# Elementwise work moved from VectorE to GpSimd, and squares from ScalarE to VectorE, in a gated-loop attention with a mixture-of-experts layer

## The chip, the core and the metric

The kernel runs on one core of one Trainium2 chip. The metric is device time in microseconds (us) of one execution, the median of several. The core has five engines with a queue each: TensorE (PE in the profile; PEld are its weight loads), VectorE (DVE), ScalarE (ACT), GpSimd (POOL) and SyncE (SP, which here only issues DMAs).

## What is computed

Two layers follow each other. The first is a recurrence over 768 steps with a complex decay per channel, for 4 batches and 8 heads of 48 channels; the second sends each of the 3072 tokens to one of 8 experts.

```python
mag = np.sqrt(a_re * a_re + a_im * a_im)
scale = np.minimum(mag, 0.999) / (mag + 1e-06)
a_re_n, a_im_n = (a_re * scale, a_im * scale)
for t in range(S):
    new_re = ar * S_re - ai * S_im
    new_im = ar * S_im + ai * S_re
    kv = np.einsum('bhd,bhe->bhde', k[:, :, t], v[:, :, t])
    S_re, S_im = (new_re + kv, new_im)
    y[:, :, t] = np.einsum('bhd,bhde->bhe', q[:, :, t], S_re)
...
logits = x @ w_gate + modality_bias[modality_id]
e_idx = np.argmax(logits, axis=1)
...
h = np.maximum(x[mask] @ w1[e], 0.0)
out[mask] = gate_w[mask, None] * (h @ w2[e])
```

## The kernel before

The recurrence is done in chunks of 128 steps: 6 chunks of each of 4 batches are 24 units, taken two at a time as 12 *pairs* (index x, `NX` = 12; a unit of the pair is `w`, `NU` = 24, and unit w is chunk `w // 4` of batch `w % 4`). A tile of a pair has 128 steps on the partitions and 2 × 8 × 48 = 768 channels in a row, in fp32.

For each pair, the decays become a phase and a log-modulus, both summed over the steps of the chunk by matmuls with triangular matrices. The steps are functions:

- `load_a` loads a_re and a_im into `abs_`, which holds two pairs.
- `squares` makes `sq` = the squares of both (ScalarE, L135, recorded at the helper's line L107 as `sq<-abs`, 1536 elements), `tan` = a_re·a_im (VectorE, L137), `neg` = the sign of a_re as bf16 (L139), and the sum of the squares (L140).
- `logs` and `tangents`: logarithms and exponentials on ScalarE; VectorE multiplies `tan` (L159) and clips `lm` (L160). `arctans` follows on ScalarE.
- `angles`: TensorE sums `tan` and `neg` into `u` (L172, L173). `fractions`: VectorE reduces it to a fraction of a turn (`f` and `r`, L193 to L202; L193 reads PSUM). `waves`: ScalarE makes sine and cosine into `css`.
- `sums` and `moduli`: TensorE sums the log-moduli, ScalarE makes `pm`, the exponential of the sum and of its negative.

For each unit, `hats` scales k and q by `pm` into `qkp` (L253) and multiplies that with the waves into `QK` (L257, 1536 elements); `turned` transposes QK on TensorE and copies it out on ScalarE (L275); `inner` makes the masked products `W` (L291, from PSUM), and the state of the recurrence: `mid` = old state + first half (L302), `U` = mid + second half (L307), both reading PSUM, and the next state = U times the chunk's decay `mt` (L309). `outer` and `rows` make the output rows and router logits (`lg`, L345). The state of a unit is read by the unit four later, the next chunk of its batch.

The loop over w (L399) writes these steps interleaved: pair x + 5 is squared while pair x + 3 gets its waves and unit w goes through `outer`. Instructions are put on the engines by a scheduler that keeps this order roughly; ScalarE's activations are kept in an exact order by `act` and `table` (L98 to L107), since each change of function table costs a load (L104). Each engine takes its queue in order. From the ninth unit on the router is made in between; from the 19th, the expert layer's first tiles. GpSimd issues the scatters of rows by token (L639, `x_slots`) and later those of the output (L885); SyncE issues the other transfers. Before 159 us of the profile GpSimd has only memsets and constants, all within the first 10 us.

Of the kernel before, what the change touches and what calls it, by code (L numbers as in the profile page):

```python
# [11 lines left out]
F32 = mybir.dt.float32  # L12
BF16 = mybir.dt.bfloat16
AX = mybir.AxisListType
Alu = mybir.AluOpType
# [8 lines left out]
def gate_loop(nc, ctx, tc, cpool, ident, q, k, v, a_re, a_im, sel, lg, x_rows, make_router, make_layers):  # L24
# [100 lines left out]
    def load_qk(x):  # L125
        qk = io.tile([L, 2, NG, H, D], F32, name="qk")
        for i, (g, b) in enumerate(groups[x]):
            nc.sync.dma_start(out=qk[:, 1, i], in_=at(q, g, b))
            nc.sync.dma_start(out=qk[:, 0, i], in_=at(k, g, b))
        box["qk", x] = qk  # L130

    def squares(x):
        ab = box.pop(("ab", x))
        sq = el.tile([L, 2, NG, H, D], F32, name="sq", bufs=1)
        act(sq[:], ab, Act.Square)  # L135
        tan = el.tile([L, NG, H, D], F32, name="tan", bufs=2)
        nc.vector.tensor_tensor(tan[:], ab[:, 0], ab[:, 1], Alu.mult)  # L137
        neg = el.tile([L, NG, H, D], BF16, name="neg", bufs=2)
        nc.vector.tensor_scalar(neg[:], ab[:, 0], 0.0, None, Alu.is_lt)  # L139
        nc.vector.tensor_tensor(sq[:, 1], sq[:, 0], sq[:, 1], Alu.add)  # L140
        box["squares", x] = sq, tan, neg
# [100 lines left out]

    def hats(w):

        if not 0 <= w < NU or (hats, w) in done:
            return
        done.add((hats, w))
        x, i = w // NG, w % NG
        cs = box["cs", x]
        pm = box["pm", x]  # L250
        qk = box["qk", x]
        qkp = un.tile([L, 2, H, D], F32, name="qkp", bufs=1)
        nc.vector.tensor_tensor(qkp[:], qk[:, :, i], pm[:, :, i], Alu.mult)  # L253
        QK = QKs[w % 4]
        wave = cs[:, i].rearrange("p h c d -> p (h c d)")[:, None, :].broadcast_to([L, 2, H * 2 * D])
        twice = qkp[:].rearrange("p a h d -> p (a h) d")[:, :, None, :].broadcast_to([L, 2 * H, 2, D])
        box["hat"] = nc.vector.tensor_tensor(QK[:, :, :, :, 0:D].rearrange("p a h c d -> p (a h c) d"), wave, twice, Alu.mult)  # L257
        box["hats", order[w]] = QK
# [22 lines left out]
    def inner(g, b):  # L281
# [23 lines left out]
        if more:  # L305
# [3 lines left out]
            nc.vector.tensor_tensor(new[:], U[:], box["mt", (g * B + b) // NG][:, b % NG, :, None].broadcast_to([C, H, D]), Alu.mult)  # L309
# [89 lines left out]
    for w in range(-4, NU + 1):  # L399
# [20 lines left out]
        if even:  # L420
# [6 lines left out]
            phase(moduli, x + 2)  # L427
            phase(logs, x + 4)
# [600 lines left out]
```

## Time and profile before

| | us |
|---|---|
| time before, median of 3 runs | 338.72 (337.75 to 339.82) |
| the profiled execution's own time | 337.64 |
| its span in the profile | 336.0 |
| busy: TensorE matmuls | 260.6 |
| busy: VectorE | 238.1 |
| busy: ScalarE | 235.6 |
| busy: GpSimd | 73.6 |
| mean granted TensorE clock | 0.938 |

The span is what the trace covers; the execution's own time is 1.6 us more. A row of a group gives the line, the engine, the operation, output and inputs with partitions × elements, the count, and after the bar the busy time in us and the mean of one in ns; then the idle time before it, with what ended that. A row of a timeline begins with its start and its duration in us. VectorE's and ScalarE's durations overlap a little with the next instruction's. A row of the view by stretches gives start and end, length, busy time and count of each engine, then the granted clock.

### The profile page before, as it was taken

What the parts mean: (1) busy time and instruction counts of PE and PEld (TensorE: products, weight loads), DVE (VectorE), ACT (ScalarE), POOL (GpSimd) and SP (SyncE); (2) the same over time, 40 slices, a digit from 0 to 9 for tenths busy, and PEclk for the clock granted to TensorE, in tenths of its full rate; (3) what the DMA queues carried; (4) which work ended last, traced back from release to release, by engine and by line L of the source; (5) the groups of instructions that cost most, each with busy time, mean ns of one, the idle gap of its engine ahead of it and who ended that gap; (6) DMA issues with size and microseconds to landing.
All of it is one profiled execution on the core that took longest, in us unless ns stands there. A gap on an engine that the chain in (4) does not pass through costs nothing.

```text
span 336.0 us, 13516 instructions
## 1 busy us (share of the span) xinstructions
PE 260.6 (78%) x5876; PEld 202.7 (60%) x5876; DVE 238.1 (71%) x437; ACT 235.6 (70%) x291; POOL 73.6 (22%) x110
## 2 busy tenths in 40 slices
PE   0034769789879798797958879899699999999960
PEld 0011448648478676676756667788678767676730
DVE  1719899999998989999897868978424373446510
ACT  2786999899998999979796978555333546542420
POOL 8100000000000000000333122324016267833440
PEclk9998596979998999997999999799989999999995
DMA  8996877869989878787989872463823441445320
GB/s 133 187 187 105 165 153 120 143 88 154 191 149 177 168 133 179 133 166 150 196 172 195 152 158 60 72 128 76 111 49 94 113 142 61 130 112 129 87 93 7
DMA packets 172157, 43.83 MB, mean 130 GB/s; under 512 B 162978, under 2 KB 168484, under 8 KB 172088
## 3 DMA queue, kind: packets, MB, share of 16 engines
q1 hardware_dynamic: 166456, 32.60, 55.3%
q0 software_dynamic: 5632, 10.26, 12.5%
q8 instruction: 48, 0.79, 1.0%
q14 instruction: 21, 0.17, 0.1%
HBM read 33.96 MB, written 9.77 MB: 130 GB/s over the span
## 4 chain that ended last, share of the span: by engine, by line
PE 42%; DVE 18%; ACT 14%; issue 9%; DMA 7%; SPq 6%; POOL 1%; POOLq 0%; DVEq 0%; ACTq 0%
PE h_ps L849 9%; PE y_ps L869 7%; PE wp L290 5%; PE up L298 4%; PE yp L327 4%; DVE QK L257 3%; ACT sq L107 3%; PE xw L339 2%; PE u L172 2%; PE ls L218 2%; ACT L104 2%; ACT pm L107 2%; PE tQT L274 2%; PE yp L321 2%; PE tKT L274 2%
## 5 line engine op out<-in xcount | busy, mean ns | idle before, releaser
L639 POOL DMA_INDIRECT x_slots<-xr,to x24 | 30.6, 1276 | 215.8 <-DMA mt<-m_scr 149.3
L172 PE MATMUL u<-tan,turn 128*128 128x384 f32 x48 | 24.3, 594 | 23.8 <-ACT tan L107 23.6
L257 DVE TENSOR_TENSOR QK<-css,qkp 128x1536 f32<-128x1536 f32 x24 | 42.1, 1755 | 0.4
L849 PE MATMUL h_ps<-xgT,w1t 128*128 128x256 bf16 (+1 forms) x312 | 36.8, 274 | 0.3 <-DMA xgT<-x_slots 0.3
L869 PE MATMUL y_ps<-w2t,hT 128*128 128x384 bf16 x200 | 35.7, 326 | 0.8 <-ACT hT L852 0.3
L885 POOL DMA_INDIRECT out_dram<-y_sb,idx x25 | 26.7, 1070 | 29.9 <-ACT y_sb L883 15.6
L849 PEld LDWEIGHTS <-w1t 128*128 128x128 bf16 x312 | 29.8, 100 | 5.6 <-issue 0.5
L104 ACT ACT_TABLE_LOAD x25 | 32.1, 1283 | 1.4 <-PEq L1013 0.9
L290 PE MATMUL wp<-QT,KT 128*64 128x64 f32 x768 | 30.8, 239 | 2.4 <-issue 1.7
L298 PE MATMUL up<-V,QK 64*64 64x48 f32 x1408 | 30.6, 234 | 2.3 <-DVE W L291 1.6
L290 PEld LDWEIGHTS wp<-QT,KT 128*64 128x64 f32 x768 | 27.2, 150 | 8.6 <-issue 2.8
L883 ACT ACTIVATE y_sb<-y_ps,own 128x384 f32<-128x384 f32 x25 | 13.2, 578 | 26.3 <-PE y_ps L869 18.3
L275 ACT COPY KT<-tKT 128x1024 f32<-128x1024 f32 x24 | 24.3, 1012 | 9.5 <-PE tKT L274 9.5
L298 PEld LDWEIGHTS up<-V,QK 64*64 64x64 f32 x1408 | 27.7, 149 | 4.3 <-DVE W L291 1.7
L852 ACT ACTIVATE hT<-h_ps 128x1024 bf16<-128x1024 f32 (+1 forms) x20 | 20.1, 1003 | 14.4 <-PE h_ps L849 14.4
L274 PE MATMUL tKT<-ident,QK 64*128 64x64 f32 x384 | 18.4, 240 | 13.0 <-DVE QK L257 10.6
L274 PEld LDWEIGHTS tKT<-ident,QK 64*128 64x128 f32 x384 | 15.2, 149 | 20.0 <-issue 16.5
L869 PEld LDWEIGHTS <-hT 128*128 128x128 bf16 x200 | 18.0, 98 | 14.6 <-DVE hT L854 2.4
L172 PEld LDWEIGHTS u<-tan,turn 128*128 128x128 f32 x48 | 9.2, 218 | 28.5 <-issue 26.0
L328 ACT COPY yT<-yp 128x512 f32<-128x512 f32 x24 | 14.0, 584 | 17.5 <-PE yp L327 17.3
L275 ACT COPY QT<-tQT 128x1024 f32<-128x1024 f32 x24 | 24.5, 1021 | 0.0
L253 DVE TENSOR_TENSOR qkp<-qk,pm 128x768 f32<-128x768 f32 x24 | 22.8, 952 | 0.3 <-ACT pm L107 0.3
(153 smaller groups left out, 542.2 us busy)
## 6 DMA issues: line engine op xcount, KB each, us to landing
abs<-in_a_re_dram SPq DMA_DIRECT2D x24, 192.0 KB
abs<-in_a_im_dram SPq DMA_DIRECT2D x24, 192.0 KB
qk<-in_q_dram SPq DMA_DIRECT2D x24, 192.0 KB
qk<-in_k_dram SPq DMA_DIRECT2D x24, 192.0 KB
V<-in_v_dram SPq DMA_DIRECT2D x24, 192.0 KB
cb<-f_scr SPq DMA_DIRECT2D x10, 384.0 KB
x_rows<-xr SPq DMA_DIRECT2D x24, 96.0 KB
abs<-in_moe_w_dram POOLq DMA_DIRECT2D x2, 768.0 KB, 8.9
```

The lines of the kernel that those rows point to most:

```text
L104: then(nc.scalar.preload_act_table_set(name))
L172: nc.tensor.matmul(us[:, i], turn[:], tan[:, i], start=True, stop=False)
L253: nc.vector.tensor_tensor(qkp[:], qk[:, :, i], pm[:, :, i], Alu.mult)
L257: box["hat"] = nc.vector.tensor_tensor(QK[:, :, :, :, 0:D].rearrange("p a h c d -> p (a h c) d"), wave, twice, Alu.mult)
L274: nc.tensor.transpose(tp[:, s, h], QK[rows_, i, h].rearrange("t c d -> t (c d)"), ident[rows_, rows_])
L275: box["turned QK"] = nc.scalar.copy(to[:], tp)
L290: nc.tensor.matmul(wp[rows_, h, :], KT[:, s, h], QT[:, s, h], start=True, stop=True)
L298: nc.tensor.matmul(up[to_c, s, h], QK[rows_, 0, h, c], V[rows_, h, 0:D], start=True, stop=True)
L639: put = self.nc.gpsimd.indirect_dma_start(out=self.x_slots, out_offset=bass.IndirectOffsetOnAxis(ap=to, axis=0), in_=self.xr[m // 4 * 4][: ...
L849: nc.tensor.matmul(h_ps[:, f // nf, f % nf, :], w1t[:, k, ff * 128:(ff + 1) * 128], xgT[:, k, :], start=(k == 0), stop=(k == KD - 1))
L869: nc.tensor.matmul(y_both[:, s], self.hT[n][:, f, s * 128:(s + 1) * 128], w2t[:, f, :], start=(f == 0), stop=(f == NF - 1))
L885: sc = self.put = nc.gpsimd.indirect_dma_start(out=self.out, out_offset=bass.IndirectOffsetOnAxis(ap=idx[:, s], axis=0), in_=y_sb[:], in_o ...
```

## The change

From the fourth pair on (x of 3 and more), `tan` and `neg` are made by GpSimd, and the squares by VectorE instead of ScalarE (the first three pairs keep theirs). The scaling of q and k becomes a function of its own, `scaled`, which overwrites `qk` in place, with the tile's axes exchanged so that one unit's k and q lie side by side; for odd units from the fourth pair on GpSimd makes it, as soon as `pm` is there, for the others VectorE does at its old place. The tile `qkp` is gone. The next state (U times decay) is made by GpSimd from the third unit on.

```diff
     def load_qk(x):
-        qk = io.tile([L, 2, NG, H, D], F32, name="qk")
+        qk = io.tile([L, NG, 2, H, D], F32, name="qk")
...
     def squares(x):
...
-        act(sq[:], ab, Act.Square)
+        if x < 3:
+            act(sq[:], ab, Act.Square)
+        else:
+            nc.vector.tensor_tensor(sq[:], ab, ab, Alu.mult)
...
-        nc.vector.tensor_tensor(tan[:], ab[:, 0], ab[:, 1], Alu.mult)
+        (nc.gpsimd if x >= 3 else nc.vector).tensor_tensor(tan[:], ab[:, 0], ab[:, 1], Alu.mult)
...
-        nc.vector.tensor_scalar(neg[:], ab[:, 0], 0.0, None, Alu.is_lt)
+        (nc.gpsimd if x >= 3 else nc.vector).tensor_scalar(neg[:], ab[:, 0], 0.0, None, Alu.is_lt)
...
+    def scaled(w):
+
+        if not 0 <= w < NU or (scaled, w) in done:
+            return
+        done.add((scaled, w))
+        x, i = w // NG, w % NG
+        pm, qk = box["pm", x], box["qk", x]
+        (nc.gpsimd if x >= 3 and w % 2 else nc.vector).tensor_tensor(qk[:, i], qk[:, i], pm[:, :, i], Alu.mult)
...
     def hats(w):
...
-        qkp = un.tile([L, 2, H, D], F32, name="qkp", bufs=1)
-        nc.vector.tensor_tensor(qkp[:], qk[:, :, i], pm[:, :, i], Alu.mult)
+        scaled(w)
...
     def inner(g, b):
...
-            nc.vector.tensor_tensor(new[:], U[:], box["mt", (g * B + b) // NG][:, b % NG, :, None].broadcast_to([C, H, D]), Alu.mult)
+            (nc.gpsimd if g * B + b >= 2 else nc.vector).tensor_tensor(new[:], U[:], box["mt", (g * B + b) // NG][:, b % NG, :, None].broadcast_to([C, H, D]), Alu.mult)
...
             phase(moduli, x + 2)
+            if x + 2 >= 3:
+                scaled(2 * x + 5)
             phase(logs, x + 4)
```

7 lines of the change are left out of this document (3 added, 4 removed).

## The prediction

> **What bounds the kernel now.** I read the page first (busy shares, the chain that ended last), then busy time by stretches cut where one pair of chunks gives way to the next (at the sum of squares, L140), then the groups by line, then the timeline of VectorE and GpSimd.
>
> ```profile
> PE 260.6 (78%) x5876; PEld 202.7 (60%) x5876; DVE 238.1 (71%) x437; ACT 235.6 (70%) x291; POOL 73.6 (22%) x110
> PE 42%; DVE 18%; ACT 14%; issue 9%; DMA 7%; SPq 6%; POOL 1%; POOLq 0%; DVEq 0%; ACTq 0%
> ```
> ```profile
> core 0: us, PE busy (x) PEld busy (x) DVE busy (x) ACT busy (x) POOL busy (x), PEclk, DMA share, GB/s
> 43.00:58.00 15.00, 11.64 (x282) 9.75 (x282) 14.06 (x20) 14.89 (x18) 0.00 (x0) 0.77 0.81 149
> 58.00:73.10 15.10, 11.78 (x245) 7.95 (x245) 14.26 (x19) 13.36 (x16) 0.00 (x0) 0.89 0.68 99
> 73.10:88.80 15.70, 13.78 (x417) 10.73 (x415) 15.37 (x27) 15.59 (x19) 0.00 (x0) 1.00 0.94 174
> 88.80:105.30 16.50, 14.24 (x426) 12.14 (x427) 16.04 (x24) 16.39 (x22) 0.00 (x0) 0.90 0.90 177
> 105.30:123.20 17.90, 16.14 (x494) 12.95 (x495) 16.25 (x24) 16.57 (x21) 0.00 (x0) 1.00 0.81 152
> 123.20:141.80 18.60, 15.16 (x460) 12.20 (x459) 17.53 (x32) 18.08 (x22) 0.00 (x0) 1.00 0.78 154
> 141.80:159.70 17.90, 15.17 (x430) 12.44 (x430) 17.55 (x47) 15.42 (x21) 0.33 (x1) 0.90 0.83 152
> 159.70:179.90 20.20, 15.01 (x459) 12.06 (x455) 18.12 (x35) 17.83 (x21) 7.64 (x7) 1.00 0.92 179
> 179.90:240.00 60.10, 52.87 (x1627) 44.81 (x1626) 44.62 (x98) 38.88 (x52) 15.53 (x14) 0.97 0.67 122
> ```
>
> The page's shares of 70% hide two regimes. From 43 to 180 us eight pairs pass, and in each VectorE and ScalarE are both nearly full: 15.37 and 15.59 of 15.70 us, 16.04 and 16.39 of 16.50. GpSimd does nothing there until 159 us. Later VectorE is busy 44.62 of 60.10 us and TensorE 52.87. So the change acts on the eight pairs, and relief of one of the two full engines counts only as far as the other follows.
>
> **What it removes.** Durations by shape, and a piece of one pair to see how instructions follow each other:
>
> ```profile
> L257 DVE TENSOR_TENSOR QK<-css,qkp 128x1536 f32<-128x1536 f32 x24 | 42.1, 1755 | 0.4
> L253 DVE TENSOR_TENSOR qkp<-qk,pm 128x768 f32<-128x768 f32 x24 | 22.8, 952 | 0.3 <-ACT pm L107 0.3
> L107 ACT ACTIVATE sq<-abs 128x1536 f32<-128x1536 f32 x12 | 17.8, 1484 | 5.9 <-DMA abs<-in_a_im_dram 5.7 <-DVE tan L159 0.2
> L291 DVE TENSOR_TENSOR W<-wp,mask 128x512 f32<-128x512 f32 x24 | 16.5, 686 | 7.9 <-PE wp L290 7.9
> L137 DVE TENSOR_TENSOR tan<-abs 128x768 f32<-128x768 f32 x12 | 11.4, 952 | 2.0 <-ACT QT L275 1.2 <-DMA abs<-in_a_im_dram 0.5 <-DMA cb<-f_scr 0.3
> L309 DVE TENSOR_TENSOR state<-U,mt 128x384 f32<-128x384 f32 x20 | 11.1, 553 | 0.1
> L139 DVE TENSOR_SCALAR neg<-abs 128x768 bf16<-128x768 f32 x12 | 7.9, 658 | 7.3 <-DMA abs<-in_a_re_dram 7.3
> L345 DVE TENSOR_REDUCE lg<-xw 128x8 f32<-128x64 f32 x24 | 5.3, 219 | 13.5 <-ACT xr L344 13.5
> ```
> ```profile
> 123.18 0.96 DVE L140 TENSOR_TENSOR sq<-sq 128x768 f32<-128x768 f32 x1 [0.63 <-ACT sq L107]
> 124.06 0.55 DVE L309 TENSOR_TENSOR state<-U,mt 128x384 f32<-128x384 f32 x1
> 125.46 0.23 DVE L345 TENSOR_REDUCE lg<-xw 128x8 f32<-128x64 f32 x1 [0.85 <-ACT xr L344]
> 125.67 0.96 DVE L137 TENSOR_TENSOR tan<-abs 128x768 f32<-128x768 f32 x1
> 126.55 0.95 DVE L193 TENSOR_TENSOR f<-u,cb 128x768 f32<-128x768 f32 x1
> 127.41 0.55 DVE L139 TENSOR_SCALAR neg<-abs 128x768 bf16<-128x768 f32 x1
> ```
>
> tan starts at 125.67, f at 126.55, neg at 127.41: an instruction of 0.95 us holds the engine 0.87, so 0.08 overlaps. In these steps 768 elements of two tensors cost 0.87, a 0.55 row (neg, or 384 elements) 0.47, W 0.60, QK 1.67, lg 0.14.
>
> A pair on VectorE now: seven of 0.87 (sum of squares, tan's product and its rescale, two on f, two scalings), four of 0.47 (neg, lm, two on r), six of 0.47 on the state (mid, U, state, twice), two W, two QK, two lg: 6.09 + 1.88 + 2.82 + 1.20 + 3.34 + 0.28 = 15.6 us. Per pair the change takes off tan's product 0.87, neg 0.47, the odd chunk's scaling 0.87 and two states 0.94, together 3.15, and adds squares of 1536 elements of two SBUF inputs, the size of QK, 1.67. Net −1.48, leaving 14.1. ScalarE loses its Square, 1.48 long, about 1.4 in steps. TensorE's instruction order is the same in both programs.
>
> **What it adds on GpSimd.** Per pair: one product (tan), one comparison (neg), one scaling, two states. No row of the trace has an elementwise product there; its nearest rows are small, and they also show what happens when the two engines meet:
>
> ```profile
> L991 POOL COPY sel<-ident 48x192 f32<-48x192 f32 x2 | 0.7, 336 | 0.1
> L52 POOL COPY mask<-mask 64x64 f32<-64x64 f32 x2 | 0.5, 232 | 0.1
> L54 POOL TENSOR_SCALAR half<-mask 128x128 f32<-128x128 f32 x1 | 0.5, 544 | 0.1
> L56 POOL CAST halfb<-half 128x128 bf16<-128x128 f32 x1 | 0.3, 293 | 0.0
> ```
> ```profile
> 1.42 0.28 POOL masks.py:199 TENSOR_SCALAR_AFFINE_SELECT ident<-ident 128x128 f32<-128x128 f32 x1
> 6.20 1.92 POOL L90 MEMSET QK<- 128x512 f32 x4
> 6.90 1.82 DVE L139 TENSOR_SCALAR neg<-abs 128x768 bf16<-128x768 f32 x1 [6.90 <-DMA abs<-in_a_re_dram]
> 8.64 0.94 DVE L137 TENSOR_TENSOR tan<-abs 128x768 f32<-128x768 f32 x1
> 9.01 0.72 POOL L525 TENSOR_SCALAR_AFFINE_SELECT tri<-ones 128x128 bf16<-128x128 bf16 x1
> 9.51 1.04 DVE L140 TENSOR_TENSOR sq<-sq 128x768 f32<-128x768 f32 x1
> 271.77 0.96 DVE L807 COPY w2t<-css 128x3072 bf16 x1
> 271.78 0.99 POOL L877 COPY idx<-own 128x2 int32 x1
> 275.40 0.23 POOL L877 COPY idx<-own 128x2 int32 x1
> ```
>
> Price. 128 more elements cost a copy 336 − 232 = 104 ns, 0.81 ns each, with 0.18 us fixed. A product reads two tensors; at two such reads 768 elements take 0.18 + 2 × 0.62 = 1.43 us and 384 take 0.80. These are estimates; the bounds are one read (0.80 for 768) and the tensor_scalar row stretched in proportion (0.544 × 6 = 3.3). neg is one read, 0.80, plus the 0.25 by which tensor_scalar exceeds the cast of the same size: 1.05, bounds 0.80 and 3.3. I take the two-read model because two copies of different size fit it and nothing else has two sizes. Per pair: 2 × 1.43 + 1.05 + 2 × 0.80 = 5.5 us. The Trainium skill ("GPSIMD Engine Reference", section 3.1) gives 4497 ns for a two-tensor add of 2048 elements; by it the product would be an estimated 1.69 and the pair 6.1, and the forecast some 4 us higher. No run here shows that yet.
>
> Meeting. neg took 1.82 us instead of 0.55 while four memsets ran on GpSimd: it ended 0.6 us after the last of them, so it got in between none. The affine_select took 0.72 instead of 0.28: it started under tan and ended 0.22 after tan's successor began, and that successor took 1.04. The two-element copy took 0.99 beside VectorE's 0.96 copy, 0.23 alone. So they exclude each other, whoever comes second. This is what the Trainium skill states ("SBUF — State Buffer", Who interferes with whom): a VectorE instruction in a two-port mode or with two SBUF inputs, and a GpSimd instruction that reads SBUF, hold the shared port in turn, whole instructions at a time. Three meetings here agree; two long products meeting, no row shows.
>
> What of the 5.5 us is hidden? VectorE's instructions with a PSUM input (W, mid, U, the first on f) and its pauses. By the new instruction order a pair runs so: the odd chunk's U releases its state on GpSimd (0.80) while VectorE goes on to lm and the squares, which read SBUF. The even chunk's U releases state, tan and neg back to back (0.80 + 1.43 + 1.05 = 3.28), while VectorE has lg, a pause as the 0.85 above, and f from PSUM (0.87), then stops at r. The scaling (1.43) becomes ready with the even one that VectorE itself makes. Hidden: about 1.5 behind the even U and 0.2 elsewhere. Some 3.8 us per pair fall on VectorE, against 1.48 saved.
>
> Sum. VectorE needs 14.1 + 3.8 = 17.9 per pair, and with 0.4 of pauses left (the 0.63 before L140 goes, since it waited for the Square) 18.3. Pair lengths: 43 to 58 has only tan and neg moved, +0.6. 58 to 73.1 has no scaling yet, 18.3 − 1.4 = 16.9 for 15.1, +1.8. 73.1 to 88.8, +2.6; 88.8 to 105.3, +1.8. The four from 105.3 last 17.9 to 20.2 already, with pauses that swallow most; +0.5 each, +2.0. After 180 us VectorE has a quarter of its time free, 0. Together +8.8: 337.64 + 8.8 = 346.5 us, the profiled execution (span 336.0) being 1.1 under the median of the runs.
>
> Costed at nothing: scaling in place keeps q and k until QK is made, 1.67 longer, and the next load of that buffer waits as long; it is asked for two pairs ahead. If that cover fails it costs at most 1.67 once per pair, as a start of QK. The layout of qk changes no size. On GpSimd's queue the scatters of rows (1.0 to 1.7 each) now stand between states and scalings from 159 us; the states are read four chunks later, the scaling a chunk later. If a scatter's wait for W or a row copy holds a scaling beyond that, QK and TensorE wait.
>
> **Rivals.** First, *faster*: the port costs less than it saves. It decides where under 1.48 us per pair falls on VectorE, that is where 4.0 of 5.5 hide; VectorE has 4.2 us per pair from PSUM (two W, four of mid and U, one f: 1.2 + 1.88 + 0.87 = 3.95, and lg), so it is possible if GpSimd's work happens to drift under them, or if two tensor reads cost as one (then GpSimd needs 2 × 0.80 + 0.80 + 2 × 0.49 = 3.4). Both full engines then shed work, and pairs shrink by 0.7 on average: 8 × 0.7 = 5.6, 332 us; with nothing blocked, 1.4 each, 326.5. For it: ScalarE is full too and surely gets its 1.4. Against it: neg at 6.90 waited out four instructions.
>
> Second, *much slower*: products nearer the stretched tensor_scalar, say 2.4 for 768 and 1.2 for 384: 9.6 on GpSimd, 7.9 on VectorE, 22.4 per pair; +6 in the two fullest pairs, about +3.5 in the others from 58 on, near 365. The page's rate stands between, at 350.5.
>
> Third, *GpSimd's queue*: in 159 to 240 us scalings held behind scatters, four odd chunks by 2 to 3 us: +8 to +12 on top or alone, 346 to 358.
>
> Fourth, *nothing*: saved and blocked balance, 338.
>
> **How the numbers follow.** Port cost as summed: 0.43. Much slower 0.11, queue 0.08; together slower 0.62. Faster 0.30, of which 0.08 under 331. Balanced, 0.08; within 0.5% (1.7 us) is what a measurement here can tell from no change. The range 331 to 358 leaves out the 0.08 and about 0.10 of the heavy cases. The likeliest case alone spans 341 to 352, from GpSimd's price.
>
> **What would show it.** In the profile after: products on GpSimd of 1.4 to 1.7 us where undisturbed; VectorE's r, scaling, squares and QK rows stretched by 0.5 to 2 us while GpSimd runs, W, mid and U not; pairs between 58 and 105 of 17 to 18.5 us; ScalarE with new pauses there. It is wrong if VectorE's rows keep 0.95 and 1.75 us while GpSimd is busy, if GpSimd's rows stretch in their place, or if the pairs get shorter.

## The result, and the profile after

The changed kernel takes 357.94 us (median of 4 runs, 356.13 to 360.01); the kernel before took 338.50 beside it (4 runs, 337.75 to 339.82). The ratio is 1.0572 [1.0498, 1.0646]: slower by 19.4 us, where the prediction had 8.8 and a range up to 358. The profiled execution took 356.84 us, 19.2 more than the 337.64 of before. Chips differ: the kernel before took 338 to 345 us on those used below. Ratios are therefore taken on one chip, against the kernel before; times are compared within the first pair of traces, unless a run is named. Delays are read at the row copies (`xr` on ScalarE, one per unit, units counted from 0). From unit 20 to 23 every trace from a chip of 344 to 345 us falls 4 to 6 us further behind the trace before, whatever its change (e3 5.1, e12 4.3, e16 4.6), and those from the other chips 1.0 at most; so times of named runs on such chips are compared only ahead of unit 20.

Busy time and the chain that ended last, from the page of the changed kernel:

```profile
PE 265.5 (75%) x5876; PEld 207.2 (58%) x5876; DVE 256.8 (72%) x401; ACT 224.8 (63%) x282; POOL 154.5 (44%) x155
PE 35%; DVE 26%; DMA 12%; issue 9%; SPq 9%; ACT 5%; POOL 1%; DVEq 0%; POOLq 0%; ACTq 0%
```

GpSimd has 80.9 us more than before, VectorE 18.7 us more although the change took net work off it, ScalarE 10.8 less. In the chain VectorE's share rises from 18 to 26% and the DMA's from 7 to 12%, ScalarE's falls from 14 to 5%: ScalarE, relieved, has left the chain, and VectorE has taken its place.

Busy time by stretches, cut at the first step of the fraction `f`, one pair each and then the rest (columns as before: length, busy time of TensorE, its loads, VectorE, ScalarE, GpSimd, the granted clock, DMA):

```profile
43.90:63.00 19.10, 14.35 (x324) 11.02 (x322) 18.89 (x22) 15.25 (x18) 6.35 (x4) 0.91 0.77 143
63.00:74.90 11.90, 8.02 (x234) 6.13 (x230) 11.72 (x15) 11.54 (x15) 2.97 (x2) 1.00 0.55 70
74.90:96.50 21.60, 15.78 (x398) 12.85 (x400) 21.07 (x27) 15.76 (x20) 8.00 (x6) 0.76 0.93 171
96.50:116.70 20.20, 17.91 (x462) 14.84 (x464) 18.11 (x19) 15.40 (x19) 8.68 (x7) 0.83 0.70 130
116.70:135.40 18.70, 16.32 (x464) 13.44 (x466) 17.83 (x20) 15.40 (x19) 7.85 (x5) 0.91 0.75 140
135.40:154.80 19.40, 15.73 (x475) 12.63 (x476) 19.23 (x30) 15.55 (x20) 8.14 (x7) 1.00 0.77 146
154.80:176.20 21.40, 17.00 (x466) 14.00 (x462) 19.68 (x41) 15.40 (x19) 11.12 (x8) 0.84 0.87 161
176.20:196.50 20.30, 16.39 (x482) 12.97 (x482) 20.09 (x34) 15.46 (x21) 14.81 (x11) 1.00 0.82 154
196.50:256.00 59.50, 51.70 (x1585) 43.91 (x1585) 45.83 (x92) 39.33 (x51) 30.79 (x21) 0.94 0.57 110
```

VectorE fills 18.89 of 19.10, 21.07 of 21.60, 19.23 of 19.40 us, and has 2.1 and 1.7 us free in the fourth and the seventh pair; ScalarE has 3 to 6 us free in all but the second pair. In the kernel before, the same cuts lie at 42.14, 58.91, 72.25, 90.31, 108.64, 126.55, 144.34, 163.28 and 183.12. The start is 1.8 us late, the first four pairs take 6.3 more, the last four 5.3 more. VectorE is busy 69.8 us in the first four and 76.8 in the last four; in the kernel before it was 63.1 and 68.7. From there to the first tiles of the expert layer the delay grows by 4.8 us, 3.8 of them between the row copies of units 19 and 21, and by 1.0 in the rest: together 19.2.

The groups by line. GpSimd's four operations first, then VectorE's rows that meet them, then one that reads PSUM:

```profile
L140 POOL TENSOR_TENSOR tan<-abs 128x768 f32<-128x768 f32 x9 | 17.0, 1892 | 42.2 <-PE u L176 17.2 <-PE u L175 13.9 <-DMA mt<-m_scr 11.1
L142 POOL TENSOR_SCALAR neg<-abs 128x768 bf16<-128x768 f32 x9 | 22.3, 2475 | 0.0
L253 POOL TENSOR_TENSOR qk<-qk,pm 128x768 f32<-128x768 f32 x9 | 18.6, 2064 | 18.1 <-ACT pm L107 10.0 <-issue 4.7 <-DMA qk<-in_k_dram 2.0
L319 POOL TENSOR_TENSOR state<-U,mt 128x384 f32<-128x384 f32 x18 | 17.4, 966 | 67.5 <-DVE U L317 64.8 <-PE yp L331 2.7
L267 DVE TENSOR_TENSOR QK<-css,qk 128x1536 f32<-128x1536 f32 x24 | 46.9, 1955 | 0.3
L253 DVE TENSOR_TENSOR qk<-qk,pm 128x768 f32<-128x768 f32 x15 | 20.1, 1354 | 0.1
L138 DVE TENSOR_TENSOR sq<-abs 128x1536 f32<-128x1536 f32 x9 | 18.1, 2015 | 0.0
L197 DVE TENSOR_SCALAR r<-f 128x768 f32<-128x768 f32 x10 | 10.9, 1089 | 0.4
L198 DVE TENSOR_TENSOR f<-f,r 128x768 f32<-128x768 f32 x10 | 11.5, 1154 | 0.2
L301 DVE TENSOR_TENSOR W<-wp,mask 128x512 f32<-128x512 f32 x24 | 16.3, 679 | 8.3 <-PE wp L300 8.3
```

QK means 1955 ns (1755 before), the scaling left on VectorE 1354 (952), r at L197 1089 and f at L198 1154; W, from PSUM, has 679 (686). One steady pair, VectorE and then GpSimd:

```profile
116.72 0.96 DVE L196 TENSOR_TENSOR f<-u,cb 128x768 f32<-128x768 f32 x1 [1.05 <-PE u L176]
117.71 1.19 DVE L197 TENSOR_SCALAR r<-f 128x768 f32<-128x768 f32 x1
118.93 1.46 DVE L198 TENSOR_TENSOR f<-f,r 128x768 f32<-128x768 f32 x1
120.43 0.87 DVE L205 TENSOR_SCALAR r<-f 128x768 int32<-128x768 int32 x1
121.22 0.67 DVE L301 TENSOR_TENSOR W<-wp,mask 128x512 f32<-128x512 f32 x1
121.81 2.20 DVE L253 TENSOR_TENSOR qk<-qk,pm 128x768 f32<-128x768 f32 x1
128.13 2.25 DVE L138 TENSOR_TENSOR sq<-abs 128x1536 f32<-128x1536 f32 x1
```
```profile
116.66 1.82 POOL L140 TENSOR_TENSOR tan<-abs 128x768 f32<-128x768 f32 x1 [1.16 <-PE u L175]
118.45 2.43 POOL L142 TENSOR_SCALAR neg<-abs 128x768 bf16<-128x768 f32 x1
121.37 1.83 POOL L253 TENSOR_TENSOR qk<-qk,pm 128x768 f32<-128x768 f32 x1 [0.48 <-POOL neg L142]
127.68 1.08 POOL L319 TENSOR_TENSOR state<-U,mt 128x384 f32<-128x384 f32 x1 [4.48 <-DVE U L317]
```

Undisturbed, r is 0.55, f 0.95, the scaling 0.95 and the squares 1.74 long. r waits out tan (to 118.48), the last r waits out neg (to 120.88), the scaling waits out GpSimd's scaling (to 123.20), the squares a state. The stretches add up to 0.64 + 0.51 + 0.32 + 1.25 + 0.51 = 3.2 us, against 1.48 saved. Only neg does not hold throughout: f − r, 1.46 long, ran wholly beside it.

GpSimd's queue where the last units meet the scatters of rows, with the expert layer's first load; first the kernel before, then the changed one with two scatters and a state left out, and at its end the two steps by which the chain that ended last leaves this queue:

```profile
229.22 1.16 POOL L639 DMA_INDIRECT x_slots<-xr,to  x1 [0.30 <-issue]
231.63 0.93 POOL L783 DMA_DIRECT2D css<-in_moe_w_dram  x1 [1.24 <-DVE QK L257]
232.32 0.39 SPq L819 DMA_DIRECT2D own<-x_slots  x1
```
```profile
237.14 2.63 POOL L253 TENSOR_TENSOR qk<-qk,pm 128x768 f32<-128x768 f32 x1 [5.17 <-ACT pm L107]
239.92 2.39 POOL L651 DMA_INDIRECT x_slots<-xr,to  x1 [0.16 <-issue]
247.47 0.95 POOL L795 DMA_DIRECT2D css<-in_moe_w_dram  x1
248.72 1.01 POOL L651 DMA_INDIRECT x_slots<-xr,to  x1 [0.30 <-issue]
```
```profile
248.72 7.08 DMA x_slots<-xr,to
256.07 0.39 SPq L831 DMA_DIRECT2D own<-x_slots  x1
```

The 16th scatter, 229.22 in the trace before, starts at 248.72, behind a scaling of 2.63 us, three scatters and a state. A load of weights (`css`, 768 KB), which stood behind this scatter before, now stands ahead of it; the scatter lands 7.08 us later and only then releases the expert layer's first load (`own`, 256.07 instead of 232.32).

### The profile page after: what moved, and what is told of

It reads as the page before. It is cut to its first block, busy times and chain, and to the rows that moved or that the text cites. A ratio compares the mean times of both kernels' runs of the same rounds, so it can differ in the third digit from the quotient of the medians.

```text
span 355.2 us, 13557 instructions
## 1 busy us (share of the span) xinstructions
PE 265.5 (75%) x5876; PEld 207.2 (58%) x5876; DVE 256.8 (72%) x401; ACT 224.8 (63%) x282; POOL 154.5 (44%) x155
## 4 chain that ended last, share of the span: by engine, by line
PE 35%; DVE 26%; DMA 12%; issue 9%; SPq 9%; ACT 5%; POOL 1%; DVEq 0%; POOLq 0%; ACTq 0%
DVE QK L267 7%; PE h_ps L861 7%; PE y_ps L881 6%; PE wp L300 5%; DVE qk L253 4%; PE up L308 3%; SPq L832 3%; PE u L175 3%; DMA xgT<-x_slots 3%; PE ls L221 2%; PE yp L337 2%; DMA V<-in_v_dram 2%; DMA qk<-in_q_dram 2%; DMA x_slots<-xr,to 2%; PE tQT L284 2%
## 5 line engine op out<-in xcount | busy, mean ns | idle before, releaser
L267 DVE TENSOR_TENSOR QK<-css,qk 128x1536 f32<-128x1536 f32 x24 | 46.9, 1955 | 0.3
L319 POOL TENSOR_TENSOR state<-U,mt 128x384 f32<-128x384 f32 x18 | 17.4, 966 | 67.5 <-DVE U L317 64.8
L651 POOL DMA_INDIRECT x_slots<-xr,to x24 | 37.2, 1548 | 21.2 <-DVE to L620 10.1
L175 PE MATMUL u<-tan,turn 128*128 128x384 f32 x48 | 22.7, 559 | 24.2 <-ACT tan L107 22.1
L300 PE MATMUL wp<-QT,KT 128*64 128x64 f32 x768 | 32.7, 249 | 5.7 <-DVE U L317 5.3
L300 PEld LDWEIGHTS wp<-QT,KT 128*64 128x64 f32 x768 | 29.1, 160 | 12.3 <-DVE U L317 6.4
L140 POOL TENSOR_TENSOR tan<-abs 128x768 f32<-128x768 f32 x9 | 17.0, 1892 | 42.2 <-PE u L176 17.2
L284 PE MATMUL tKT<-ident,QK 64*128 64x64 f32 x384 | 18.3, 240 | 19.6 <-DVE QK L267 14.5
L308 PE MATMUL up<-V,QK 64*64 64x48 f32 x1408 | 31.9, 240 | 1.3 <-issue 1.1
L308 PEld LDWEIGHTS up<-V,QK 64*64 64x64 f32 x1408 | 28.6, 155 | 3.4 <-issue 1.2
L284 PE MATMUL tQT<-ident,QK 64*128 64x64 f32 x384 | 18.4, 243 | 11.2 <-ACT yT L338 7.1
```

What stands on the lines that cost most here:

```text
L175: nc.tensor.matmul(us[:, i], turn[:], tan[:, i], start=True, stop=False)
L284: nc.tensor.transpose(tp[:, s, h], QK[rows_, i, h].rearrange("t c d -> t (c d)"), ident[rows_, rows_])
L300: nc.tensor.matmul(wp[rows_, h, :], KT[:, s, h], QT[:, s, h], start=True, stop=True)
L308: nc.tensor.matmul(up[to_c, s, h], QK[rows_, 0, h, c], V[rows_, h, 0:D], start=True, stop=True)
L651: put = self.nc.gpsimd.indirect_dma_start(out=self.x_slots, out_offset=bass.IndirectOffsetOnAxis(ap=to, axis=0), in_=self.xr[m // 4 * 4][: ...
```

## The experiments

Theory P: products on GpSimd and VectorE's rows with two SBUF inputs exclude each other, and what that takes from VectorE in the full pairs is the loss. Theory W: the loss is in waits for results that come later from the slower engine. Theory Q: part of it is GpSimd's queue, where a waiting scaling stands before the scatters. Diffs are against the kernel before unless said otherwise.

### The port or the waits

**e1** repeats, beside all of VectorE's own work, the moved operations on GpSimd (704 of 768 elements, bf16) into a spare that nothing reads; the output is not affected. **e2** gives GpSimd as much to do in memsets, each series released in the same place by a copy of one element.

```diff
+        if x >= 3:                                          # e1
+            nc.gpsimd.tensor_tensor(spare[:], ab[:, 0, :, :, 0:44], ab[:, 1, :, :, 0:44], Alu.mult)
+            nc.gpsimd.tensor_scalar(spare[:], ab[:, 0, :, :, 0:44], 0.0, None, Alu.is_lt)
...
+            if g * B + b >= 2:
+                nc.gpsimd.tensor_tensor(spare[:], U[:], box["mt", ...], Alu.mult)
...
+            if 3 <= x + 2 < NX:
+                nc.gpsimd.tensor_tensor(spare[:], box["qk", x + 2][...], box["pm", x + 2][...], Alu.mult)
```
```diff
+            nc.gpsimd.tensor_copy(spare[:, 0, 0:1], ...)     # e2
+            for _ in range(10):                              # 2 after U, 4 after pm
+                nc.gpsimd.memset(spare[:], 0.0)
```

> The kernel before, unchanged, and beside it GpSimd makes the product, the comparison, the odd chunk's scaling and the state once more, at the places of the changed kernel, into a spare tile that nobody reads (704 of 768 elements; the state whole). VectorE still makes all of them. Theory P (the shared port): VectorE's rows that read two SBUF tensors or run in a two-port mode stretch as in the changed kernel, by about 3.2 us per pair; VectorE then needs 15.6 + 3.2 = 18.8 per pair and is full everywhere up to 180 us: +3 in the pairs at 58 to 105, +1 to +2 in the others, and scatters late at the end, together +16 to +24 us, 355 to 362. Theory W (the kernel waits for GpSimd's slower results): nothing waits for the spare tile, so 338 to 342, and VectorE's rows keep 0.95, 0.55 and 1.75 us.

> The kernel before with GpSimd kept busy about as long per pair (sixteen to eighteen memsets of 352 elements, some 0.35 us each), at the same places, each series behind a copy of one element. Memsets write SBUF and read nothing. Theory P in the narrow form (it is the read side that product and product exclude each other on): the rows with two SBUF inputs keep 0.95 and 1.75 us; only neg, lm and r (0.55 us) stretch, by 0.5 to 2 us each, four per pair but few of them meeting a series: +1 to +2 us per pair on VectorE, 343 to 350. Theory P in the wide form (any work of GpSimd stops VectorE): as much as the unread copies, 355 to 362. Theory W: 338 to 341.

Measured: e1 1.0705 [1.0613, 1.0797], e2 1.0092 [1.0039, 1.0144]. The groups by line of e1, then of e2:

```profile
L262 DVE TENSOR_TENSOR QK<-css,qkp 128x1536 f32<-128x1536 f32 x24 | 44.8, 1868 | 0.4
L314 DVE TENSOR_TENSOR state<-U,mt 128x384 f32<-128x384 f32 x20 | 18.9, 946 | 0.1
L312 DVE TENSOR_TENSOR U<-mid,up 128x384 f32<-128x384 f32 x20 | 11.0, 549 | 0.7
```
```profile
L263 DVE TENSOR_TENSOR QK<-css,qkp 128x1536 f32<-128x1536 f32 x24 | 42.1, 1754 | 0.4
L145 POOL MEMSET spare<- 128x352 f32 x90 | 40.2, 446 | 5.1 <-POOL spare L142 0.2
L315 DVE TENSOR_TENSOR state<-U,mt 128x384 f32<-128x384 f32 x20 | 11.0, 552 | 0.1
```

Nothing waits for the results in e1, yet QK is stretched from 1755 to 1868 ns and the state from 553 to 946, while U, from PSUM, keeps 549: P holds, and W isn't needed for a loss of this size (Q may be part of it: e1's products stand between the scatters too). W isn't seen in the changed kernel either: in its trace no wait of VectorE, ScalarE or TensorE is ended by an elementwise row of GpSimd. With memsets, 90 of 446 ns at one place alone, QK and the state keep 1754 and 552, so it is GpSimd's reading that excludes them. This is what the Trainium skill states ("SBUF — State Buffer", Who interferes with whom): a two-input row contends with a GpSimd instruction that reads SBUF and not with one that only writes; by it these rows of e2 are free, and the trace agrees. Only r, with one input, is stretched somewhat by memsets (555 to 619 ns and 556 to 638). e2's loss of 0.9% is less than the 343 us asked for the narrow form (1.3%) and a little above the range of W; the rows decide here, not the time. Of the three meetings that the prediction counted, the one of neg with memsets is therefore of another kind, since memsets read nothing.

### One part at a time

Five kernels make one part of the change each: **e4** the squares on VectorE, **e6** the states, **e7** tan and neg, **e8** only the scaling in place (all on VectorE, odd units' right after `pm`), **e10** that with the odd units' scaling on GpSimd. **e3** is the changed kernel with everything of GpSimd's put back on VectorE.

```diff
-        act(sq[:], ab, Act.Square)                                   # e4
+        if x < 3:
+            act(sq[:], ab, Act.Square)
+        else:
+            nc.vector.tensor_tensor(sq[:], ab, ab, Alu.mult)
...
+            (nc.gpsimd if g * B + b >= 2 else nc.vector)...          # e6: new state
+        (nc.gpsimd if x >= 3 else nc.vector)...                      # e7: tan and neg
+        nc.vector.tensor_tensor(qk[:, i], qk[:, i], pm[:, :, i], Alu.mult)             # e8
+        (nc.gpsimd if x >= 3 and w % 2 else nc.vector).tensor_tensor(qk[:, i], ...)    # e10
```

> The changed kernel with the four GpSimd steps back on VectorE: squares on VectorE and scaling in place stay. Theory P: VectorE needs 15.6 + 1.67 = 17.3 us per pair with no stretched row, against 17.3 with the stretches in the changed kernel (14.1 + 3.2): about as slow as the changed kernel in the pairs up to 180 us, less the late part on GpSimd's queue (4 us): 346 to 354. Theory W: without waits for GpSimd it loses only what VectorE's 1.67 costs, and ScalarE's relief pays part of it: 338 to 345.

> The kernel before with the squares alone on VectorE from the fourth pair. VectorE 15.6 + 1.67 = 17.3 per pair, ScalarE 1.4 less. Both theories: VectorE becomes the bound in the pairs at 43 to 105 us: +1.7 there in three to four pairs, +0.5 in the four later ones: 343 to 349. If ScalarE was what set the pairs (rival), no change or a gain: 335 to 339. The difference to the run with scaling in place is what in-place and early scaling cost.

> The kernel before with the states alone on GpSimd, from the third unit on. VectorE is relieved of 2 x 0.47 per pair; a state takes 0.83 us on GpSimd and stops a VectorE instruction on two SBUF inputs by up to that. Theory P: the odd chunk's state costs VectorE about 0.5, the even one's is hidden behind lg and f: net -0.4 per pair, 0.99 to 1.00 before the scatters, and 1 to 4 us lost on GpSimd's queue afterwards: 0.99 to 1.01. Theory W (states late for the unit four later): slower by more than 1%, with mid waiting for GpSimd.

> The kernel before with tan and neg alone on GpSimd from the fourth pair on; squares stay on ScalarE. VectorE is relieved of 1.34 per pair; tan holds the read side 1.8 us and neg, 2.4 us long, part of that. Theory P: stretches of 1.5 to 3 us per pair: 1.00 to 1.03. Without the port: 0.97 to 0.99, since VectorE loses 1.34 of 15.6 per pair.

> The kernel before with the scaling in place, odd units' early, all on VectorE; nothing on GpSimd, squares on ScalarE. The run with squares and scaling in place was 1.1% faster than the one with squares alone, which says 0.985 to 0.995; if that was a chance of the order of instructions: 1.00, 0.997 to 1.005.

> The kernel before with scaling in place, the odd units' on GpSimd from the fourth pair on, nothing else moved. VectorE is relieved of 0.87 per pair; the scaling lasts 1.83 us on GpSimd and meets the even unit's scaling, which in the changed kernel lasted 2.1 to 2.2 instead of 0.95. Theory P: +0.3 to +0.4 us per pair, and GpSimd's queue late by up to 4 us at the expert layer: 1.005 to 1.025. If the queue doesn't matter: 1.00 to 1.01.

| | ratio to before |
|---|---|
| e3 all on VectorE | 1.0128 [1.0035, 1.0221] |
| e4 squares alone | 1.0243 [1.0161, 1.0324] |
| e6 states alone | 0.9976 [0.9920, 1.0033] |
| e7 tan and neg alone | 1.0119 [1.0036, 1.0203] |
| e8 scaling in place | 1.0009 [0.9962, 1.0055] |
| e10 odd scaling on GpSimd | 1.0407 [1.0335, 1.0479] |

e8: the in-place layout costs nothing, as forecast. e3: VectorE there is busy 248.6 us; the moved operations take some 28 us of it in steps (18 × 0.87 of tan and scaling, 9 × 0.47 of neg, 18 × 0.47 of states), so that 220 would be left, and the changed kernel has 256.8. So some 36 us of its VectorE time are stretch (32 when reckoned from the kernel before): the move gave back more than it took. e3's time itself, though, lies in the range given for W and under that for P: 17.3 us of VectorE's steps per pair, with no GpSimd beside them, cost 1.3% and not 2.2 or more. e4: the squares on VectorE cost 2.4% by themselves, although ScalarE, just as full, is relieved; that e3, with the squares and the in-place scaling, loses less than e4 is not explained, and the intervals overlap. The single parts add up to 7.5% where the whole has 5.7; with intervals of 0.6 to 0.8 on each, that may be chance. e10 missed its expectation, and it is the costliest part; I had thought of the scaling as one product like tan.

### Parts taken back from the changed kernel

**e5** puts the states from unit 12 and the scalings from the tenth pair back on VectorE, **e9** the squares on ScalarE, **e11** tan and neg of the fourth and fifth pair on VectorE.

```diff
-        (nc.gpsimd if x >= 3 and w % 2 else nc.vector).tensor_tensor(qk[:, i], ...)    # e5
+        (nc.gpsimd if 3 <= x < 9 and w % 2 else nc.vector).tensor_tensor(qk[:, i], ...)
-            (nc.gpsimd if g * B + b >= 2 else nc.vector).tensor_tensor(new[:], ...)
+            (nc.gpsimd if 2 <= g * B + b < 12 else nc.vector).tensor_tensor(new[:], ...)
...
-        if x < 3:                                                                      # e9
-            act(sq[:], ab, Act.Square)
-        else:
-            nc.vector.tensor_tensor(sq[:], ab, ab, Alu.mult)
+        act(sq[:], ab, Act.Square)
...
-        (nc.gpsimd if x >= 3 else nc.vector).tensor_tensor(tan[:], ...)                # e11; neg alike
+        (nc.gpsimd if x >= 5 else nc.vector).tensor_tensor(tan[:], ...)
```

> The changed kernel with the states from the thirteenth unit on and the odd scalings from the tenth pair on back on VectorE, so that none of them stands between the scatters of rows on GpSimd's queue (tan and neg stay there to the last pair). Theory Q (the last 4 to 5 us of the loss come from the sixteenth scatter, held on GpSimd's queue behind a scaling that waits for pm): the delay against the kernel before stays what it is up to 180 us, some 12 us, and does not grow by 4 at the expert layer's start; 1.025 to 1.04 of the time before. Rival: the delay at the start of the expert layer only hands on what the chunks lost, and it stays at 1.05 to 1.06.

> The changed kernel with the squares back on ScalarE; all four steps stay on GpSimd. Theory P: VectorE then needs 14.1 - 1.67 + 2.7 (the stretches without the squares' own 0.5) = 15.2 us per pair, under the 15.6 of the kernel before, and ScalarE is as full as before: no loss in the steady pairs; what stays is the start (tan and neg alone: +2 to +4 us) and GpSimd's queue at the end (+4): 1.01 to 1.03. Rival (GpSimd's work costs by itself, whatever VectorE has to spare): 1.045 to 1.06, as the changed kernel.

> The changed kernel with tan and neg on GpSimd from the sixth pair on instead of the fourth. In the changed kernel two of them fall into the start, where VectorE's tan took 2.41 and a state 2.06 us beside them. If the start costs: 2 to 3 us less than the changed kernel, 1.045 to 1.052. If the start is made up for later: as the changed kernel, 1.055 to 1.06.

Measured: e5 1.0286 [1.0193, 1.0380], e9 1.0395 [1.0305, 1.0485], e11 1.0522 [1.0435, 1.0609]. In e5 the row copies are 11.4 us late at unit 11 and 9.6 to 9.9 at units 20 to 23, where the changed kernel goes from 13.5 to 18.2: the growth at the end is gone, and the 16th scatter starts at 239.64. About half of the loss, then, goes with GpSimd's scalings and states after unit 12. In e9 the delay at unit 9 is 6.5 us where the changed kernel has 11.4, but the 16th scatter still starts at 245.20; it missed the 1.03 expected at most. e11 recovers the start (4 us at unit 3) and has given back all but 1.2 of it by unit 19; the intervals don't tell it from the changed kernel.

### GpSimd's queue

**e14** makes only the three last odd scalings (tenth to twelfth pair) on GpSimd, **e13** only the six before them, **e15** is the changed kernel without the last three.

```diff
+        (nc.gpsimd if x >= 9 and w % 2 else nc.vector).tensor_tensor(qk[:, i], ...)        # e14
+        (nc.gpsimd if 3 <= x < 9 and w % 2 else nc.vector).tensor_tensor(qk[:, i], ...)    # e13
-        (nc.gpsimd if x >= 3 and w % 2 else nc.vector).tensor_tensor(qk[:, i], ...)        # e15, against the changed kernel
+        (nc.gpsimd if 3 <= x < 9 and w % 2 else nc.vector).tensor_tensor(qk[:, i], ...)
```

> The complement: the odd scaling on GpSimd for pairs 9 to 11 alone, three instructions in all. Theory Q: most of the loss, 1.02 to 1.03, with the sixteenth scatter 6 us or more later than the rows of its unit. Theory P alone: three of nine, at most 1.013.

> The kernel before with scaling in place, the odd units' on GpSimd for pairs 3 to 8 alone, so that only the last of them stands near the scatters. Theory Q (the larger part of the 4% of the odd scaling on GpSimd comes from the last three, which wait for pm with scatters behind them): only the port's part is left, 6 x 0.5 = 3 us, 1.005 to 1.013, and the sixteenth scatter is no later than the units' rows are. Theory P alone (each scaling costs the same): six ninths of 4.1%: 1.02 to 1.03.

> The changed kernel with the odd scalings of the last three pairs alone back on VectorE; the states stay on GpSimd's queue among the scatters. With states and late scalings back it had 1.029. If the scalings, which wait for pm, hold the scatters: 1.028 to 1.04. If the states do as well: 1.045 to 1.055.

Measured: e14 1.0279 [1.0172, 1.0386], e13 1.0196 [1.0121, 1.0271], e15 1.0358 [1.0289, 1.0427]. GpSimd's timeline in e14:

```profile
226.69 2.62 POOL L250 TENSOR_TENSOR qk<-qk,pm 128x768 f32<-128x768 f32 x1 [10.88 <-issue]
229.47 2.36 POOL L648 DMA_INDIRECT x_slots<-xr,to  x1 [0.17 <-issue]
235.76 1.65 POOL L792 DMA_DIRECT2D css<-in_moe_w_dram  x1 [1.17 <-DVE QK L264]
237.71 1.01 POOL L648 DMA_INDIRECT x_slots<-xr,to  x1 [0.30 <-DVE mid L309]
```

At units 13 to 15 its row copies are 0.6 to 0.8 us late; then GpSimd stands 10.88 us before the scaling (pm ends at 226.54), the scatters queue behind it, and the 16th comes at 237.71 instead of 229.22. Of this delay 3.6 us are in unit 16's row copy already, ahead of that scaling, behind a stretch of half clock from 214 to 220 us. Three instructions that save VectorE 0.87 us each cost 2.8% alone; taking them out of the changed kernel gives 2.1 of its 5.7%. Q holds, for the scalings, though e13 lies above its range (1.005 to 1.013) and just under that of P alone. The late states, by e5 against e15, add 0.7%, which the intervals don't tell from nothing.

What a waiting scaling costs has two parts that no run separates. In all six traces with the late scalings on GpSimd (the changed kernel, e9, e10, e11, e14, e17), and in e18, the load of weights stands ahead of the 16th scatter, and the expert layer's first load goes out 6.9 to 8.0 us after the start of that scatter. In the other thirteen the weights come behind the scatter, and the first load follows after 2.7 to 4.4 us. So some 4 us come with the order of the scatter and the weights, and not with the scaling's length or its wait.

### Why the early scalings cost 2%

e13 was not explained: its scaling row on VectorE has a mean of 1267 ns over 18, a stretch of 18 × 0.32 = 5.7 us, and r at L202 has 686 instead of 556, another 1.6; together little more than the 6 × 0.87 = 5.2 that it saves. **e16** lets each of the six wait for the even unit's QK, so that it can't meet the even unit's scaling, which QK and the transposes wait for.

```diff
+        made = (nc.gpsimd if 3 <= x < 9 and w % 2 else nc.vector).tensor_tensor(qk[:, i], ...)
+        if 3 <= x < 9 and w % 2:
+            tc.add_manual_dep(made.ins, box["hat"].ins.name, ...)
...
+            if 6 <= n + 3 < 18:
+                scaled(n + 4)
```

> The kernel before, with the odd units' scaling of pairs 3 to 8 on GpSimd as in e13, but each of the six waits for the even unit's QK on VectorE, so that it can't meet the even unit's own scaling. Theory chain: the 2.0% of e13 came from the even scaling being stretched (1267 ns mean where 950 is the undisturbed length) at the place where QK and TensorE's transposes wait for it; with the meeting moved behind QK that row goes back to about 950 ns and the ratio to at most 1.01. Theory amount: what counts is how much VectorE time is taken, wherever it is taken; then other rows of VectorE (squares, r, tan) are stretched by as much, 0.5 to 1.5 us a pair, and the ratio stays at 1.015 to 1.025. A third reading, that the odd unit's QK now waits for GpSimd (some 1.8 us, issued late), would show as a pause before the odd QK with GpSimd's scaling as what ended it, and a ratio of 1.02 or more.

Measured: 1.0281 [1.0228, 1.0334], a little above the range of the theory of the amount. The groups by line:

```profile
L250 DVE TENSOR_TENSOR qk<-qk,pm 128x768 f32<-128x768 f32 x18 | 16.8, 950 | 0.3 <-ACT pm L107 0.3
L159 DVE TENSOR_TENSOR tan<-tan,sq 128x768 f32<-128x768 f32 x12 | 18.9, 1577 | 2.5 <-ACT sq L107 2.5
```

The even scaling is back at 950 ns, as intended, and the rescale of tan (952 before) has 1577 instead: 12 × 0.63 = 7.5 us. The meeting moved and the loss stayed, so the theory of the chain falls; no pause before the odd QK appeared, so the third reading falls too. But 7.5 − 5.2 = 2.3 us of VectorE's time are not 2.8%, some 9 us, either. TensorE shows something more. Stretches of 2.5 us in the changed kernel's third pair, and a group of transposes and a row of VectorE in it:

```profile
82.50:85.00 2.50, 0.19 (x4) 0.19 (x6) 2.50 (x4) 2.26 (x4) 0.97 (x1) 0.67 0.94 180
85.00:87.50 2.50, 0.93 (x16) 0.74 (x14) 2.50 (x5) 1.52 (x2) 0.00 (x1) 0.50 1.26 215
87.50:90.00 2.50, 2.44 (x42) 2.35 (x44) 2.50 (x2) 1.61 (x3) 1.08 (x1) 0.50 1.06 265
90.00:92.50 2.50, 2.50 (x85) 2.38 (x85) 2.50 (x4) 2.48 (x3) 0.00 (x0) 0.50 0.96 188
92.50:95.00 2.50, 2.50 (x81) 2.15 (x78) 2.50 (x4) 0.94 (x3) 0.00 (x0) 0.78 0.77 89
```
```profile
84.81 1.11 PE L284 MATMUL tKT<-ident,QK 64*128 64x64 f32 x16 [3.17 <-DVE W L301]
```
```profile
81.73 1.96 DVE L556 TENSOR_TENSOR bias<-bias,bias_m 128x192 f32<-128x192 f32 x1
```

The bias row at 81.73, 0.35 us long in the kernel before, waits out GpSimd's scaling (81.62, 1.85 long) and takes 1.96; two short rows ahead of it (76.07 and 77.53) had taken 1.8 us more than before while tan and neg ran. W behind them is late, TensorE stands 3.17 us for W, and the clock is at 0.50 from some 83.3 to some 93.6 us, where sixteen transposes take 1.11 us instead of 0.71. That pair lost 3.5 us, the most of all; but one QK of 1.75 us lies before the pair's first cut in the kernel before (69.19) and behind it here (78.93), so that half of these 3.5 us is work of the second pair, which gained 1.4. The Trainium skill states such a rule ("TensorE: Matmul & The Clock Gate", Part 1: half clock after an idle window of some 3.4 us, full clock again after a busy one). The trace shows the fall and the return, but not these lengths: the clock fell some 1.7 us into the pause, and came back after some 6 us of a busy TensorE.

How much of it is VectorE's time? The eight pairs from the first cut at `f` to the ninth, in us; the last column sums (1 − clock) over stretches of 2.5 us from 40 to 215:

| | length | VectorE busy | VectorE free | lost clock share |
|---|---|---|---|---|
| before | 141.0 | 131.8 | 9.2 | 10.7 |
| changed | 152.6 | 146.6 | 6.0 | 18.3 |
| e3, all on VectorE | 142.7 | 141.5 | 1.2 | 12.9 |
| e8, scaling in place | 141.6 | 131.5 | 10.2 | 11.5 |
| e9, squares back | 146.8 | 132.9 | 13.9 | 15.4 |
| e13, six scalings | 147.3 | 136.1 | 11.2 | 16.6 |
| e16, the six moved | 149.1 | 136.3 | 12.8 | 16.0 |

In e3 VectorE has 9.7 us more to do than before, and its pauses take up all but 1.7. Where products run on GpSimd they don't: in e9 VectorE is busy 1.1 us more and the pairs last 5.8 longer, half of the changed kernel's 11.6. So the loss in the pairs is not the amount of VectorE's time alone. Whether the rest comes from the place where a row is stretched or from TensorE's clock, which is lower in each of these runs, the table can't tell.

Does the clock add to the delay or only follow it? **e17** and **e18** fill TensorE's pauses in the changed kernel and in the kernel before with products whose results are overwritten; the output is not affected.

```diff
             tp = pair([C, H, L // 2], "t" + name)
+            for _ in range(3 if box.setdefault("turns", 0) >= 12 else 0):
+                nc.tensor.matmul(tp[:, 0]..., ident[:, 0:C], turn[:], start=True, stop=True)
+            box["turns"] += 1
```

> The changed kernel with added work on TensorE: from the seventh unit on, three products of 128 x 128 ahead of the transposes of K and three ahead of those of Q, whose results the transposes overwrite; about 0.5 us each three at the full clock, 1 us per unit. The trace of the changed kernel has half-clock stretches (0.50 to 0.58 for 2.5 to 7.5 us) behind pauses of TensorE; between 40 and 215 us the shares lost add up to 18.3 us against 10.7 before. Theory clock: part of the 19 us is the clock, which falls when the delayed VectorE leaves TensorE idle; filled pauses then keep the clock up, the lost share falls to 11 or less, and the ratio comes down from 1.057 to 1.03 to 1.045. Theory no amplifier: the time is set by VectorE and GpSimd's queue, the clock only follows; the lost share falls but the ratio stays at 1.05 to 1.065. If TensorE's own time bounds the stretches between the pauses, the added 18 x 1 us shows in full, 1.08 or more.

> The kernel before with the same added products on TensorE. It has five half-clock stretches between 40 and 215 us, 10.7 us of lost share. Theory clock: a lower loss and a ratio of 0.985 to 1.00. Theory no amplifier: 1.00 to 1.01 where the pauses take them in, and up to 1.05 where TensorE's time bounds.

Measured: e17 1.0814 [1.0727, 1.0902], e18 1.0445 [1.0374, 1.0515]. Both lie where TensorE's own time was taken to bound. The filling cost more than I put it at: TensorE is busy 293.9 us in e18 where it had 260.6, 1.8 us per unit and not 1. It raised the clock (lost share 7.7 us in e18; 13.5 in e17, where 11 or less was expected), and still both are slower than without it. With the filling on both sides the change costs 1.0814 / 1.0445 = 1.035, without it 1.057. That is what the clock theory asks for, but a kernel with longer pauses takes the filling more easily whatever the clock does, and in e18 the load of weights went ahead of the 16th scatter as it does in the changed kernel, which costs the kernel before something that the changed one had paid already. How much of the 19 us the clock makes stays open.

### A version that might gain

**e12** keeps the part that cost nothing, the states, for units 2 to 11, and puts half the squares of five pairs on VectorE.

```diff
+        if x < 4 or x > 8:
             act(sq[:], ab, Act.Square)
+        else:
+            act(sq[:, 0], ab[:, 0], Act.Square)
+            nc.vector.tensor_tensor(sq[:, 1], ab[:, 1], ab[:, 1], Alu.mult)
...
+            (nc.gpsimd if 2 <= g * B + b < 12 else nc.vector).tensor_tensor(new[:], ...)
```

> An attempt at a faster version: the kernel before with the states on GpSimd for units 2 to 11 alone, and of the squares of pairs 4 to 8 those of a_im alone on VectorE. Per pair VectorE loses 0.94 and gains 0.87 and about 0.5 of stretch, ScalarE loses about 0.65: if ScalarE sets the pairs, 5 x 0.5 = 2.5 us less, 0.99 to 0.995; if VectorE is as full, 1.00 to 1.005.

Measured: 1.0062 [1.0019, 1.0104]. No version tried beats the kernel before.

## Why the prediction was right or wrong

**Right: the mechanism and the place.** GpSimd's reading rows and VectorE's rows with two SBUF inputs exclude each other (e1, e2), and r, with one input, waits for them too. r, the scaling, QK and the squares are stretched by 0.3 to 1.6 us, W, mid and U not. The stretch in the pair shown is 3.2 us against 3.8 forecast. The first four pairs, from 42 to 109 us, lost 6.3 against 6.8, though not one by one: the third lost 3.5 and the second gained 1.4. That the sum came so near is in part luck: GpSimd's work was longer than forecast and blocked less of its length, and by e9 the loss is not made by VectorE's time alone.

**Sizes on GpSimd, too low.** The product takes 1.82 undisturbed, not 1.43; the estimate of 1.69 from the figure of the Trainium skill ("GPSIMD Engine Reference", section 3.1) was nearer. State and neg: 0.83 (0.80 forecast), and 2.43 where I had 1.05 and bounds of 0.80 to 3.3. A pair is 2 × 1.82 + 2.43 + 2 × 0.83 = 7.7, not 5.5. The stretch stayed near the forecast all the same; neg lets part of VectorE's work through (f − r ran beside it).

**The step that failed first: "pauses that swallow most" of the four later pairs, +0.5 each.** They lost 5.3 us instead of 2.0. The sum took a need of 18.3 us for each, built from 15.6 us of steps, and found it nearly covered by their length. But the prediction's own stretches have VectorE busy 16.25, 17.53, 17.55 and 18.12 us there, 17.4 on average, since from the ninth unit on the router's rows run in between, and free for 5.2 us in all four. With 3.8 − 1.48 = 2.3 us more in each, 9.3 us had to go into pauses of 5.2: at least 4.1 were left over, not 2.0. The traces show just that: VectorE's busy time in these pairs grew by 8.1 us, its pauses shrank from 5.7 to 3.0, and 5.3 remained.

How much the pauses take up does not go by the amount alone. In e3 these four pairs have 5.1 us more of VectorE's work and are 0.3 us shorter; in e9 they have 0.8 more and are 2.9 longer. In e9, with 1.67 us less on VectorE per pair than in the changed kernel, the delay grows from 5.0 us at unit 3 to 6.5 at unit 9, where the changed kernel goes from 6.7 to 11.4: VectorE's time makes about half of the loss in the pairs. What makes the other half, and the 2% of e13 and e16, is not settled.

**The step that failed second: GpSimd's queue at nothing.** The third rival (0.08) came true beside the main case: 3.8 us of the trace, and by e14 and e15 2 to 3%, some 7 to 9 us, where it had 8 to 12. Its place was as written, its direction was not: the scatters wait behind a scaling, not a scaling behind the scatters; and that the load of weights would come to stand ahead of the 16th scatter was not foreseen. To have costed it at nothing because the result is read a chunk later was to look at the wrong customer: the scatters behind it were the late ones.

**Not counted: the start.** 1.8 us by 43 us: GpSimd's first tan and neg meet VectorE's last tan (2.41 instead of 0.95); e7, which moves these two alone, is 1.6 us late at the same place.

Together: 6.3 + 5.3 + 3.8 + 1.8 + 2.0 elsewhere = 19.2, where the prediction had 6.8 + 2.0. The rivals "faster" and "nothing" fell, as the stretch is twice what is saved; "much slower" (near 365) came nearer in size than the main case, but its reason, products of 2.4 us, did not hold.

## What to carry to other kernels

In this kernel GpSimd's products passed VectorE unhindered where VectorE read PSUM, and memsets passed its rows with two inputs. So before work is moved to GpSimd, count how many microseconds of such rows there are in the full stretch, and take each meeting at up to the rest of GpSimd's instruction, however short VectorE's is. Take an engine's free time from the stretches of the profile and not from a sum of steps, which may leave rows out. Before an instruction that waits is put into a queue, look at what stands behind it there, not only at who reads its result, and whether the order of the transfers in that queue has changed. And where two engines are both full, moving work between them can starve the third, whose clock then falls; what that added here stays open.

## What the hardware showed that I had not expected

- neg, a tensor_scalar with one input of 768 elements from fp32 to bf16, takes GpSimd 2.43 us, longer than a product of two inputs (1.82); and VectorE's f − r ran beside it from start to end.
- A short VectorE row pays the whole meeting: 0.35 us became 1.96 behind one scaling.
- Among the products a scatter keeps GpSimd longer, but not each: 1.0 to 2.6 us in the changed kernel (mean 1.55 for 24), 1.0 to 2.0 before (1.28). Right behind a scaling two took 1.53 and 1.57 us and two 2.33 and 2.39.
- A load of 768 KB issued just ahead of a scatter goes with a slow scatter: 7.1 to 7.6 us to landing in the five traces where the chain that ended last runs through it. That the load is the cause was not tested.
- A pause of 3.17 us on TensorE came with some 10 us at half clock, in the middle of a kernel that keeps it 75% busy.
